# A planner's priorities from a table by the pair's place in its batch set, and high weights first in one form of the second layer

## The chip, the cores and the metric

The kernel runs on 1 core of one Trainium2 chip. The metric is device time in microseconds (us). Before the change the median of 3 runs is 901.65 us (898.36 to 903.74). The core's engines are TensorE (PE; its weight loads are listed apart as PEld), VectorE (DVE), ScalarE (ACT), GpSimd (POOL) and SyncE (SP), which here issues nearly all DMA transfers on one queue.

## What is computed

Attention with a threshold instead of a mask, then a mixture-of-experts layer on the tokens that a skip score lets through:

```python
# q, k, v: (8 batches, 8 heads, 576, 64); x: 4608 tokens of 512; 8 experts, 512 -> 1024 -> 512
scores = scale * np.matmul(q, k.transpose(0, 1, 3, 2))
thresh = np.max(scores, axis=-1, keepdims=True) - tau
scores = np.where(scores >= thresh, scores, -1000000000.0)
attn = softmax(scores)
x = (attn @ v) rearranged to tokens
do_compute = x @ w_skip > 0                  # the others leave as x
xc = x[do_compute]; logits = xc @ w_gate
e_idx = np.argmax(logits, axis=1); gate_w = softmax(logits) of that expert
for e in range(8):                            # the tokens of expert e
    h = np.maximum(xc[mask] @ w1[e], 0.0)
    y[mask] = gate_w[mask, None] * (h @ w2[e])
out[do_compute] = xc + y
```

## The kernel before

**Attention.** The work is cut into 32 pairs of heads (4 pairs a batch, 8 batches). A pair has 9 units of 128 query rows by 576 keys: four chunks of two units, and a last single unit that holds the remaining 64 rows of both heads. Each unit goes through the same steps. PE makes the scores (`S`, L537) into a PSUM tile `sps`, of which there are 3. DVE takes the row maximum (`mx`, L548), then the threshold of the chunk (`th`, L555). ACT takes the exponentials (`e`, L560). DVE compares and multiplies into `p` (`p`, L568), which frees the `sps` tile. ACT then copies a chunk's `p` as a high half in 16 bits (`ph`, L348, out `hla`), POOL subtracts to get the low half (`pl`, L619), SP sends both halves through DMA transposes (`tt`, L624, out `PTa`, 3 buffers), and PE multiplies with V (`av`, L687). The last unit is transposed on PE (L641) and split by ACT and DVE (L649, out `TM`).

**V of a batch.** SP loads it in six transfers into `vraw` (L399, L403, L406), one buffer. Two sums of its absolute values are taken (`fsum`: on DVE L432, or on ACT L430; the planner chooses the engine). From them a power of two is made (L440 to L471), by which V is scaled (L491, L494) and split into a high half `Vh` and a low half `Vl` (L502).

**Between the pairs.** SP loads q and k two pairs ahead (L373, L374, `KQ`) and ACT scales the keys (`qs`, L379). Finished token rows are stored (L858, L868). A finished pair's rows are turned on PE (L795) and multiplied with the gate's weights (L821). After every second batch DVE runs the gate (L920 to L1016, some 25 small steps) and POOL scatters the records (L1044): from pairs 10, 18 and 26 on and, for the last two batches, at the end.

**The order.** All these steps are handed to a planner (`Plan`) as operations with dependences, estimated durations, and a key. `Plan.run` goes forward in estimated time: of the operations that are ready on an engine within 0.1 us of each other, it issues the one with the smallest key. Instructions then stand on each engine in that order, and an engine that waits for one holds all behind it. The key is a number: 9 times the pair's number plus twice the chunk's, plus an offset by kind of step from the table `OFF`. The offsets lie between -6854 and 7967; the pair's part goes to 287. The gate's small steps are spread by `GS` (50.281) from one to the next.

**The experts.** At the end of attention the expert with the most tokens is chosen (L1095 to L1112), its weights are loaded (L333) and split into high and low parts (copies L350 and L348, subtractions `wl`, L1196, on DVE or POOL), its tokens are gathered (L337 with the numbers from L1148 and L1149) and turned (L1216), and its first layer runs (L1247). The code after `pl.run` is written in a fixed order: for each of the nine jobs, first layer (`layer1`, L1469), second layer (`layer2`, L1531, or for three jobs `layer2_t`, L1550, with the weights as the stationary operand), the split of the next weights (L1428 on ACT, L1429 on DVE and POOL), stores (L1509). All products are made of three: high times high, low times high, high times low.

Of the kernel before, what the change touches and what calls it, by code (L numbers as in the profile page):

```python
# [20 lines left out]
PSUM = bass.MemoryType.PSUM  # L21
# [4 lines left out]
S = 576  # L26
# [22 lines left out]
STEP = 2 * NM + 1  # L49
NBK = (NM + 1) * H + H // 2  # L50
NTL = NM * H
SPB = 3
# [7 lines left out]
TMB = 2  # L60
RING = 2
TD = 0.0
GS = 50.281
DU = 7
WRB = 4
LOOK = 0.1
# [3 lines left out]
LTO = {"PE": 0.08, "DVE": 0.0, "ACT": 0.0, "POOL": 0.01, "SP": 0.05}  # L70
DISS = 2.2
DLAT = 1.9
OFF = dict(
    gk=-2113.0, vm=619.2, tt2=3725.8, hi2=-664.7, lo2=-5330.0, eg=6314.5, L1m=-3010.0, ex=-2785.6, eav=102.1, ld=17.7, qs=-4430.6, S=-2220.1, mx=4043.6, th=-6854.0, e=-1838.1, p=-3039.7, ph=-893.6, pl=-1882.1, tt=-2108.6, av=4179.2, cp=-1831.1, x=1668.8, xw=-2128.1, row=4356.9, rsp=4714.0, init=2975.2, L1=7966.6, sc=-3459.1, d0=1027.8, phD=4238.9, v=1589.6, vsp=523.9, V2=-555.1,
)

class Op:
    def __init__(self, key, fn, eng, lat, lock):
# [16 lines left out]
class Plan:  # L95
# [7 lines left out]
        self.rings[name][1].append(list(ops))  # L103

    def op(self, key, fn, deps, eng, lat=None, lock=False):
        o = Op(key, fn, eng, lat, lock)
        for d in deps:
            if isinstance(d, tuple) and len(d) == 1:
                o.deps.append((d[0], True))
            elif isinstance(d, tuple):  # L110
                name, bufs = d
                al, fr = self.rings.setdefault(name, ([], []))
                if al:
                    o.deps.append((al[-1], True))
# [71 lines left out]
def attn_moe_kernel(ctx: ExitStack, tc: tile.TileContext, kq, vl, vt, tau, wg, w1, w2, out):  # L186
# [6 lines left out]
    cp = ctx.enter_context(tc.tile_pool(name="cp", bufs=1))  # L193
# [29 lines left out]
    att = ExitStack()  # L223
    ap_ = att.enter_context(tc.tile_pool(name="att", bufs=2))
    a1 = att.enter_context(tc.tile_pool(name="a1", bufs=1))
    ps_s = att.enter_context(tc.tile_pool(name="ps_s", bufs=SPB, space=PSUM))
    ps_t = att.enter_context(tc.tile_pool(name="ps_t", bufs=GPB, space=PSUM))
    ps_a = att.enter_context(tc.tile_pool(name="ps_a", bufs=1, space=PSUM))

    QKs = []  # L230

# [92 lines left out]
    pl = Plan()  # L324
# [1062 lines left out]
    att.close()  # L1387
    moe = ExitStack()
    mp = moe.enter_context(tc.tile_pool(name="moe", bufs=2, reuse_waits="tile"))
    ps_x = moe.enter_context(tc.tile_pool(name="ps_x", bufs=2, space=PSUM, reuse_waits="tile"))  # L1390
    ps_h = moe.enter_context(tc.tile_pool(name="ps_h", bufs=3, space=PSUM, reuse_waits="tile"))
    ps_y = moe.enter_context(tc.tile_pool(name="ps_y", bufs=3, space=PSUM, reuse_waits="tile"))

    class late:
        at, base = 0, None
# [142 lines left out]
    def layer2_t(j, w, side):  # L1538
# [2 lines left out]
        yt = mp.tile([P, NDT, TCAP], F32, name="yt", tag="yt", bufs=1)  # L1541
        for d in range(NDT):
            yp = ps_y.tile([P, 512], F32, name="yps", tag="yps")
            mm = [
                (w_[:, f, d * P : (d + 1) * P], h[:, f, 0:cap])
                for f in range(NFT)
                for (h, w_) in ((j.hh, wh), (j.hl, wh), (j.hh, wl))
            ]
            for i, (w_, h) in enumerate(mm):
                nc.tensor.matmul(yp[:, 0:cap], w_, h, start=(i == 0), stop=(i == len(mm) - 1))  # L1550
            nc.scalar.activation(yt[:, d, 0:cap], yp[:, 0:cap], AF.Copy)
            for s in side.get(d, ()):
                s()
# [130 lines left out]
    for k in range(1, len(jobs)):  # L1684
        j = jobs[k]
# [147 lines left out]
```

## Time and profile before

| | before |
|---|---|
| median of 3 runs | 901.65 us |
| lowest, highest | 898.36, 903.74 us |
| profiled execution | 897.73 us |
| its span, first to last instruction | 895.6 us |
| PE, DVE, ACT, POOL busy | 802.1, 692.3, 595.4, 573.4 us |
| mean granted TensorE clock | 0.966 |

Attention fills the first 600 us of the span, the handover to the experts lasts until 634 us, and the experts' layers run from there to the end. The profile is of one execution; it is read by stretches (busy time of each engine in a window), by waits (who waited for whom) and by engine in order of time. A wait's number is idle time of the waiting engine; it costs nothing where another engine sets the pace.

### The profile page before, as it was taken

The page shows a single profiled execution, that of the slowest core. Times are in us where ns is not written, and L with a number is a line of the kernel's source. Part 1 is how long each engine was busy: PE and PEld are TensorE (multiplying, and loading weights), DVE is VectorE, ACT ScalarE, POOL GpSimd, SP SyncE. Part 2 cuts the span into 40 slices and gives each one's busy share as a digit, 9 for nine tenths or more (in the row PEclk, how much of TensorE's full clock was granted, in tenths as well). Part 3 has the DMA queues.
Part 4 walks back from the last instruction along what each step waited for, and adds up shares of the span by engine and source line. Part 5 has one row for each costly group of instructions (what it writes and reads, how often), then busy time and mean ns, then how long its engine had stood idle before and what let it go on. Part 6 is the DMA issues. An engine that isn't in the chain of part 4 may idle for free. (4 is left out here: it accounts for less than half of the span.)

```text
span 895.6 us, 19554 instructions
## 1 busy us (share of the span) xinstructions
PE 802.1 (90%) x7294; PEld 679.0 (76%) x7294; DVE 692.3 (77%) x1294; ACT 595.4 (66%) x933; POOL 573.4 (64%) x379
## 2 busy tenths in 40 slices
PE   7799899898899888989988898975999999999997
PEld 5577787677677677777777776864968898999986
DVE  7789889989998798988888988895453554487782
ACT  5588888985987696797788779853243452454451
POOL 4567965975986494797676689756253455473463
PEclk9799999999999899999999999996799999999999
DMA  9699999999999999999999999987354635544540
GB/s 210 141 182 181 183 186 204 203 219 200 188 182 177 197 194 208 194 186 181 201 215 180 209 214 155 202 155 234 137 174 140 212 104 180 188 148 163 186 148 19
DMA packets 340031, 160.84 MB, mean 180 GB/s; under 512 B 311095, under 2 KB 311863, under 8 KB 339936
## 3 DMA queue, kind: packets, MB, share of 16 engines
q1 hardware_dynamic: 335312, 149.43, 81.8%
q0 software_dynamic: 4480, 10.15, 3.4%
q8 instruction: 59, 0.97, 0.5%
q14 instruction: 36, 0.29, 0.1%
q10 hardware_dynamic: 144, 0.00, 0.0%
HBM read 69.33 MB, written 15.21 MB: 94 GB/s over the span
## 5 line engine op out<-in xcount | busy, mean ns | idle before, releaser
L619 POOL TENSOR_TENSOR hla<-p,hla 128x1152 f16<-128x1152 f32 x128 | 304.4, 2379 | 121.5 <-ACT hla L348 109.3
L537 PE MATMUL sps<-KQ 128*128 128x288 f32 x1152 | 324.8, 426 | 37.7 <-DVE p L568 34.2
L537 PEld LDWEIGHTS sps<-KQ 128*128 128x128 f32 x1152 | 212.9, 195 | 100.6 <-PE avp L687 16.4
L560 ACT ACTIVATE ea<-sps,mx 128x576 f32<-128x576 f32 x288 | 206.8, 740 | 59.1 <-DVE mx L548 50.8
L548 DVE TENSOR_REDUCE mx<-sps 128x1 f32<-128x576 f32 x288 | 214.9, 751 | 34.7 <-PE sps L537 32.1
L568 DVE SCALAR_TENSOR_TENSOR p<-sps,tq,ea 128x576 f32<-128x576 f32 x256 | 200.1, 812 | 19.8 <-ACT ea L560 6.0
L348 ACT ACTIVATE hla<-p 128x1152 f16<-128x1152 f32 x128 | 148.8, 1162 | 29.2 <-DVE p L568 15.8
L687 PEld LDWEIGHTS <-PTa 128*128 128x128 f16 x3456 | 128.0, 99 | 36.5 <-issue 16.8
L687 PE MATMUL avp<-Vh,PTa 128*128 128x65 f16 (+1 forms) x2304 | 140.4, 199 | 16.0 <-ACT a L348 7.9
L687 PE MATMUL avp<-Vl,PTa 128*128 128x64 f16 (+1 forms) x1152 | 128.4, 198 | 6.1 <-POOL Vl L502 5.4
L1429 POOL TENSOR_TENSOR wl<-wr,wh 128x1024 fp32r<-128x1024 f32 x26 | 66.7, 2581 | 26.6 <-ACT wh L1428 18.7
L1509 POOL DMA_INDIRECT out<-o,ids x20 | 20.0, 998 | 80.8 <-DVE o L1508 27.1
L1469 PE MATMUL hps<-xh,wh 128*128 128x288 f32 (+4 forms) x224 | 69.1, 308 | 0.1
L1469 PE MATMUL hps<-xl,wh 128*128 128x288 f32 (+4 forms) x224 | 67.9, 303 | 0.0
L1469 PE MATMUL hps<-xh,wl 128*128 128x288 f32 (+4 forms) x224 | 67.8, 303 | 0.0
L1470 ACT ACTIVATE QK<-hps 128x288 fp32r<-128x288 f32 (+4 forms) x56 | 23.9, 426 | 60.8 <-PE hps L1469 60.2
L1428 ACT ACTIVATE wh<-wr 128x1024 fp32r<-128x1024 f32 x56 | 56.7, 1051 | 0.0
L1044 POOL DMA_INDIRECT lst<-rec,si x36 | 35.9, 998 | 31.6 <-DVE h L1255 17.0
L1429 DVE TENSOR_TENSOR wl<-wr,wh 128x1024 fp32r<-128x1024 f32 x30 | 50.2, 1689 | 6.9 <-ACT wh L1428 6.1
L348 ACT ACTIVATE a<-avp 64x65 f32<-64x65 f32 (+1 forms) x128 | 36.8, 301 | 20.1 <-PE avp L687 19.6
L1471 DVE SCALAR_TENSOR_TENSOR QK<-hps,QK 128x288 fp32r<-128x288 f32 (+4 forms) x56 | 26.2, 470 | 31.0 <-ACT QK L1470 29.0
L739 POOL TENSOR_TENSOR xb<-a,z 128x512 f32<-128x512 f32 x32 | 33.4, 1042 | 24.5 <-DVE z L730 10.7
(244 smaller groups left out, 1323.4 us busy)
## 6 DMA issues: line engine op xcount, KB each, us to landing
wr<-in_w SPq DMA_DIRECT2D x29, 1024.0 KB
KQ<-in_kq SPq DMA_DIRECT2D x32, 320.0 KB
KQ<-in_kq SPq DMA_DIRECT2D x32, 304.0 KB
vraw<-in_vl SPq DMA_DIRECT2D x32, 256.0 KB
out<-xb SPq DMA_DIRECT2D x32, 256.0 KB
PTa<-hla SPq DMA_TRANSPOSE x256
wn<-in_w SPq DMA_DIRECT2D x2, 1024.0 KB
vraw<-in_vt SPq DMA_DIRECT2D x8, 128.0 KB
```

The lines of the kernel that those rows point to most:

```text
L348: nc.scalar.activation(dst, src, AF.Copy)
L537: nc.tensor.matmul(ps[:, j, 0:HS], w, k[:, c0 : c0 + HS], start=True, stop=True, skip_group_check=True)
L548: nc.vector.tensor_reduce(T["mx", g][:, c, 0:1], bank(u), AX.XY, ALU.max, negate=True)
L560: nc.scalar.activation(e, bank(u), AF.Exp, bias=T["mx", g][:, c, 0:1])
L568: nc.vector.scalar_tensor_tensor(T["p", g, i][:, u].rearrange("p (a b) -> p a b", a=2), bank(u), T["tq", g][:, c : c + 1], T.pop(("e", g, ...
L619: nc.gpsimd.tensor_tensor(hl[:, lo0 : lo0 + w], T.pop(("p", g, i)).rearrange("p a b -> p (a b)"), hl[:, 0:w], op=ALU.subtract)
L687: nc.tensor.matmul(pv[:, o, 0:e], x[:, w_, :], y[:, vb, 0:e], start=not M and i % 2 + a + k == 0, stop=a == len(work) - 1 and k == 2, skip ...
L739: nc.gpsimd.tensor_tensor(T["x", b].rearrange("p c (h d) -> p c h d", d=D)[:, :, 2 * hp : 2 * hp + 2], T["a", g][:, 0:NM, :, 0:D], T["z", ...
L1044: sc = nc.gpsimd.indirect_dma_start(lst[:, :], bass.IndirectOffsetOnAxis(ap=G["si"][:, 0, t : t + 1], axis=0), G["rec"][:, t, :], None, bo ...
L1428: nc.scalar.activation(w[0][:, sl], rs, AF.Copy)
L1429: lo[q % 2].tensor_tensor(w[1][:, sl], rs, w[0][:, sl].bitcast(F32), op=ALU.subtract)
L1469: nc.tensor.matmul(hp_[:, 0:cap], w_, x, start=(i == 0), stop=(i == len(mm) - 1))
```

## The change

Four edits. First, a key no longer is a number. `OFF[kind]` gives a symbolic key, and `place` turns a sum of such keys into a priority by looking up the table `ORDER` at the pair's number modulo the length of the kind's row: rows of four depend on the pair's place in its batch, rows of two on even or odd pairs, rows of one are constant. The pair's and the chunk's number only choose the place; small additions such as `+ 0.1 * u` count no more. Keys without an `OFF` (the start, the second-layer weights, the steps planned ahead) stay numbers. Second, `GS` comes from the table as well and is 3.047e-10, so the steps of a gate share one priority. Third, the PSUM pools are opened in another order: in attention `ps_s` comes last, in the experts' stage `ps_y` first. Fourth, `layer2_t` takes all products with the high weights of an output block before those with the low weights, as `layer2` already does. No instruction is added or removed but for the planner's choice of engine for steps that can run on two.

```diff
-GS = 50.281
-OFF = dict(
-    gk=-2113.0, vm=619.2, tt2=3725.8, hi2=-664.7, ...
+ORDER = dict(
+    vm=(5384, 0, 0, 0,),
+    ld=(-3.456e+04, 1.596e+05, -1.641e+05, 6.358e+04,),
+    S=(-2.225e+05, -1.566e+05, -2.312e+04, -9.311e+04,),
...
+    GS=(3.047e-10,),
 )
+class Key:
+    def __init__(self, at=0.0, offs=()):
+        self.at, self.offs = at, tuple(offs)
...
+def place(key):
+    if not isinstance(key, Key):
+        return key
+    pair = int(max(key.at, 0)) // STEP
+    return sum(c * ORDER[n][pair % len(ORDER[n])] for n, c in key.offs) if key.offs else key.at
+OFF = {n: Key(0, [(n, 1)]) for n in ORDER}
+GS = OFF["GS"]
...
-        o = Op(key, fn, eng, lat, lock)
+        o = Op(place(key), fn, eng, lat, lock)
...
-    ps_s = att.enter_context(tc.tile_pool(name="ps_s", bufs=SPB, space=PSUM))
     ps_t = att.enter_context(tc.tile_pool(name="ps_t", bufs=GPB, space=PSUM))
     ps_a = att.enter_context(tc.tile_pool(name="ps_a", bufs=1, space=PSUM))
+    ps_s = att.enter_context(tc.tile_pool(name="ps_s", bufs=SPB, space=PSUM))
...
+    ps_y = moe.enter_context(tc.tile_pool(name="ps_y", bufs=3, space=PSUM, reuse_waits="tile"))
     ps_x = moe.enter_context(tc.tile_pool(name="ps_x", bufs=2, space=PSUM, reuse_waits="tile"))
     ps_h = moe.enter_context(tc.tile_pool(name="ps_h", bufs=3, space=PSUM, reuse_waits="tile"))
-    ps_y = moe.enter_context(tc.tile_pool(name="ps_y", bufs=3, space=PSUM, reuse_waits="tile"))
...
+            three = ((j.hh, wh), (j.hl, wh), (j.hh, wl))
             mm = [
                 (w_[:, f, d * P : (d + 1) * P], h[:, f, 0:cap])
+                for part in (three[0:2], three[2:])
                 for f in range(NFT)
-                for (h, w_) in ((j.hh, wh), (j.hl, wh), (j.hh, wl))
+                for (h, w_) in part
             ]
```

In the changed kernel all planned steps stand 64 lines further down (L399 is L463). The order of instructions differs nearly everywhere in attention; three places follow.

**SP, the load of V of batch 4** (pairs 14 and 15 before, the end of pair 12 in the change; `vraw<-in_vl` and `vraw<-in_vt` are V, `out<-xb` the stores of token rows, `PTa<-hla` transposes, `KQ` loads of q and k). Before:

```order
L624 DMA_TRANSPOSE PTa<-hla 128x9x128 x7
L403 DMA vraw<-in_vt 64x512
L406 DMA vraw<-in_vt 64x256
L624 DMA_TRANSPOSE PTa<-hla 128x9x128 x6
L399 DMA vraw<-in_vl 128x512
L624 DMA_TRANSPOSE PTa<-hla 128x9x128
L399 DMA vraw<-in_vl 128x512
L373 DMA KQ_109<-in_kq 64x1280
L374 DMA KQ_109<-in_kq 64x1216
```

and in the change:

```order
L688 DMA_TRANSPOSE PTa<-hla 128x9x128 x4
L463 DMA vraw<-in_vl 128x512 x2
L922 DMA out<-xb 128x512 x4
L467 DMA vraw<-in_vt 64x512
L470 DMA vraw<-in_vt 64x256
L463 DMA vraw<-in_vl 128x512 x2
L688 DMA_TRANSPOSE PTa<-hla 128x9x128 x14
```

The six transfers of V, which were spread over two pairs for batches 2, 4 and 6, stand together with the four stores between two transposes, for every batch from 2 to 7; the sums of V come 12 units after them where they came 6.

**DVE, the first gate** (pair 10; `ca` and `gw` are the gate's tiles, `vmx<-vraw` a sum of V, L568 the masks `p`). Before:

```order
L929 TENSOR_TENSOR ca<-lg,gw 128x72
L930 TENSOR_TENSOR ca<-lg,gw 128x72
L548 TENSOR_REDUCE mx_120<-sps 128x1
L432 TENSOR_REDUCE vmx<-vraw 128x1
L555 TENSOR_REDUCE tq_121<-mx_120 128x2
L440 TENSOR_REDUCE vmx<-vmx 128x1
L568 SCALAR_TENSOR_TENSOR p<-sps,tq_121,ea 128x576 x2
L933 TENSOR_TENSOR ca<-ca,ioem 128x72
L934 TENSOR_SCALAR gw<-lg 128x9
L972 TENSOR_REDUCE gw<-ca 128x9
L973 TENSOR_SCALAR rec<-tokp 128x9
```

and in the change:

```order
L993 TENSOR_TENSOR ca<-lg,gw 128x72
L994 TENSOR_TENSOR ca<-lg,gw 128x72
L612 TENSOR_REDUCE mx_120<-sps 128x1
L997 TENSOR_TENSOR ca<-ca,ioem 128x72
L998 TENSOR_SCALAR gw<-lg 128x9
L619 TENSOR_REDUCE tq_121<-mx_120 128x2
L1001 TENSOR_REDUCE gw<-ca 128x9
L1002 TENSOR_SCALAR gw<-gw 128x9
L632 SCALAR_TENSOR_TENSOR p<-sps,tq_121,ea 128x576 x2
L1005 TENSOR_TENSOR ca<-ioem,gw 128x9x8
```

The sum of V has left DVE here (in batches 3, 5 and 7 ACT now makes both sums, so DVE makes 5 of the 16 instead of 8), the gate begins half a pair earlier, and its steps are mixed more finely with the units' steps.

**DVE, the handover to the experts** (from the last mask `pm`, L568; `wl` are the low parts of the first expert's weights, `TM` the last unit's low half, `id` the numbers for the gather). Before:

```order
L568 SCALAR_TENSOR_TENSOR pm_117<-sps,tq_121,ea 128x576
L1196 TENSOR_TENSOR wl_8291<-wr,wh_8283 128x512
L1196 TENSOR_TENSOR wl_8309<-raw_8249,wh_8283 128x512
L1196 TENSOR_TENSOR wl_8309<-raw_8249,w_8339 128x512
L649 TENSOR_TENSOR TM_128<-sps,TM_128 128x640
L835 TENSOR_TENSOR lg<-lg,gps 128x64
L1148 CAST id_146<-rec_145 128x3
L1149 TENSOR_SCALAR id_146<-rec_145 128x3
```

and in the change:

```order
L632 SCALAR_TENSOR_TENSOR pm_117<-sps,tq_121,ea 128x576
L899 TENSOR_TENSOR lg<-lg,gps 128x64
L414 CAST wh_8246<-wr 128x512
L1260 TENSOR_TENSOR wl_8277<-wr,wh_8246 128x512
L899 TENSOR_TENSOR lg<-lg,gps 128x64
L713 TENSOR_TENSOR TM_128<-sps,TM_128 128x640
L1260 TENSOR_TENSOR wl_8356<-raw_8153,wh_8246 128x512 x2
L1260 TENSOR_TENSOR wl_8356<-raw_8153,w_8318 128x512
L1212 CAST id_146<-rec_145 128x3
L1213 TENSOR_SCALAR id_146<-rec_145 128x3
```

The last unit's low half has moved ahead of three of the subtractions, and the gather's numbers still stand behind them; POOL makes four of the eight subtractions instead of three, in a row.

## Rows read from the trace of the kernel before

**Rows 1.** Busy time by stretch: us, busy us of each engine (instructions), clock, DMA share, GB/s
```profile
200.00:300.00 100.00, 88.90 (x1002) 73.21 (x1000) 88.51 (x168) 79.28 (x123) 75.05 (x46) 0.98 1.09 189
...
600.00:650.00 50.00, 38.39 (x264) 33.91 (x263) 27.13 (x70) 15.35 (x31) 22.74 (x21) 0.71 0.61 189
...
740.00:780.00 40.00, 40.00 (x241) 35.97 (x241) 19.25 (x33) 14.99 (x26) 20.64 (x11) 1.00 0.58 194
```
**Rows 2.** Waits in attention, 30 to 600 us: who for whom, us in total, times, longest
```profile
PE sps L537 <- DVE p L568: 31.4, 46, 2.5
DVE mx L548 <- PE sps L537: 30.5, 65, 1.3
...
ACT KQ L379 <- DMA KQ<-in_kq: 14.8, 11, 3.6
...
PE avp L687 <- DMA PTa<-hla: 5.8, 8, 1.3
PE avp L687 <- POOL Vl L502: 5.4, 1, 5.4
```
**Rows 3.** Busy time by pair, columns as in rows 1: pairs 7, 10, 15, 23
```profile
138.10:156.60 18.50, 17.05 (x207) 14.34 (x206) 17.41 (x35) 16.40 (x26) 10.90 (x6) 1.00 1.09 212
...
189.00:213.30 24.30, 21.25 (x242) 17.88 (x241) 22.66 (x53) 17.37 (x29) 13.25 (x7) 0.93 1.08 193
283.30:306.50 23.20, 18.91 (x206) 15.65 (x205) 17.78 (x35) 17.10 (x29) 12.30 (x8) 0.89 1.14 182
...
434.80:455.50 20.70, 17.33 (x207) 14.38 (x206) 17.57 (x35) 16.59 (x29) 10.94 (x6) 1.00 1.16 196
```
**Rows 4.** Groups of instructions in attention: count, busy us, mean ns, idle before
```profile
L432 DVE TENSOR_REDUCE vmx<-vraw 128x1 f32<-128x1280 f32 x7 | 10.4, 1479 | 3.5 <-DMA vraw<-in_vl 3.5
...
L430 ACT ACTIVATE Vl<-vraw 128x1280 f16<-128x1280 f32 x7 | 8.8, 1262 | 0.0
```
**Rows 5.** In order of time, pair 15: SP's last load of V, and DVE and ACT
```profile
293.07 0.56 SPq L399 DMA_DIRECT2D vraw<-in_vl  x1
...
298.65 1.49 DVE L432 TENSOR_REDUCE vmx<-vraw 128x1 f32<-128x1280 f32 x1 [2.81 <-DMA vraw<-in_vl]
...
300.99 0.83 ACT L379 ACTIVATE KQ<-KQ,tpos 128x640 f32<-128x640 f32 x1 [3.59 <-DMA KQ<-in_kq]
```
**Rows 6.** In order of time: SP's longest run of transfers, PE's product; sizes (page)
```profile
178.31 0.56 SPq L858 DMA_DIRECT2D out<-xb  x1
178.97 0.87 SPq L399 DMA_DIRECT2D vraw<-in_vl  x2
...
181.18 9.30 SPq L624 DMA_TRANSPOSE PTa<-hla  x6
...
200.03 0.19 PE L687 MATMUL avp<-Vh,PTa 128*128 128x65 f16 x1
...
vraw<-in_vl SPq DMA_DIRECT2D x32, 256.0 KB
out<-xb SPq DMA_DIRECT2D x32, 256.0 KB
```
**Rows 7.** DVE, POOL and PE in order of time at the handover
```profile
608.27 7.20 DVE L1196 TENSOR_TENSOR wl<-wr,wh 128x512 fp32r<-128x512 f32 x1
...
607.87 2.40 POOL L619 TENSOR_TENSOR hla<-p,hla 128x1152 f16<-128x1152 f32 x1
...
613.88 1.04 POOL L739 TENSOR_TENSOR xb<-a,z 128x512 f32<-128x512 f32 x1
...
615.40 0.68 DVE L1196 TENSOR_TENSOR wl<-raw,wh 128x512 fp32r<-128x512 f32 x1
...
617.47 0.40 PE L687 MATMUL avp<-Vh,TM 128*128 128x130 f16 x2 [2.80 <-DVE TM L649]
...
626.39 0.93 PE L1216 MATMUL sps<-ident,xg 128*128 128x128 f32 x3
```
**Rows 8.** PE's waits in the experts' stage, 625 us to the end
```profile
PE yps L1550 <- POOL wl L1429: 1.9, 2, 1.2
```

More of the change, by code (lines that the diff above doesn't have):

```diff
@@ L72 @@
 DLAT = 1.9
-OFF = dict(
-    gk=-2113.0, vm=619.2, tt2=3725.8, hi2=-664.7, lo2=-5330.0, eg=6314.5, L1m=-3010.0, ex=-2785.6, eav=102.1, ld=17.7, qs=-4430.6, S=-2220.1, mx=4043.6, th=-6854.0, e=-1838.1, p=-3039.7, ph=-893.6, pl=-1882.1, tt=-2108.6, av=4179.2, cp=-1831.1, x=1668.8, xw=-2128.1, row=4356.9, rsp=4714.0, init=2975.2, L1=7966.6, sc=-3459.1, d0=1027.8, phD=4238.9, v=1589.6, vsp=523.9, V2=-555.1,
-)
+ORDER = dict(
+    gk=(4349, 1.58e+04, 0, 0,),
+    vm=(5384, 0, 0, 0,),
+    tt2=(613.7, 1.58e+04, -3.449e+04, -1512,),
+    hi2=(-4.346e+04, 3.034e+05, 3.133e+05, -5282,),
+    lo2=(562.8, -2.259e+04, -9.309e+04, -4.515e+04,),
+    eg=(-7406, -2.093e+05, 0, 0,),
+    L1m=(2.989e+05,),
+    ex=(-8.448e+04, 1.427e+04, -3.875e+04, -2e+04,),
+    eav=(-1.313e+05, -1.651e+04, 4.278e+04, 1.964e+04,),
+    ld=(-3.456e+04, 1.596e+05, -1.641e+05, 6.358e+04,),
+    qs=(1.122e+05, 1717, -9.452e+04, 1.214e+04,),
+    S=(-2.225e+05, -1.566e+05, -2.312e+04, -9.311e+04,),
+    mx=(5534, 2.237e+05, -6.53e+04, -6820,),
+    th=(-3.468e+04, 1.915e+05, -1.495e+05, 6.269e+04,),
+    e=(-1.451e+05, -6.782e+04, -2141, -1.003e+04,),
+    p=(-9031, -1.426e+04, -1.807e+05, -1.63e+05,),
+    ph=(-1322, 1.222e+05, 4.057e+05, -9.705e+04,),
+    pl=(-1.781e+05, 4.205e+04, 6250, -6.626e+04,),
+    tt=(-2.69e+05, 6405, -2703, 9.818e+04,),
+    av=(3.22e+05, 2.029e+04, 3.147e+04, 3.456e+04,),
+    cp=(1.287e+04, -3.512e+04, -6.049e+04, -1.725e+05,),
+    x=(-2.958e+04, -4.386e+04, 0.001192, 4.233e+04,),
+    xw=(2433, 1831, 1.558e+04, -1.251e+05,),
+    row=(-1594, 0, 0, 0,),
+    rsp=(-1.029e+05, 0, 0, 0,),
+    init=(-2.381e+05,),
+    L1=(-1.868e+05,),
+    sc=(-1.345e+05,),
+    d0=(-1.107e+04,),
+    v=(0.000848, 0, 0, -9374,),
+    vsp=(-0.0004024, 0, 0, -1.917e+05,),
+    V2=(0.002816, 0, 0, 0,),
+    GS=(3.047e-10,),
+)
@@ new lines, with __add__, __mul__, __sub__ @@
+class Key:
+    def __init__(self, at=0.0, offs=()):
+        self.at, self.offs = at, tuple(offs)
+    def __add__(self, x):
+        x = x if isinstance(x, Key) else Key(x)
+        return Key(self.at + x.at, self.offs + x.offs)
+    def __mul__(self, a):
+        return Key(self.at * a, [(n, c * a) for n, c in self.offs])
+    def __sub__(self, x):
+        return self + x * -1
+    def __rsub__(self, x):
+        return self * -1 + x
+    __radd__, __rmul__ = __add__, __mul__
+def place(key):
[3 more added lines that the diff above has]
+    return sum(c * ORDER[n][pair % len(ORDER[n])] for n, c in key.offs) if key.offs else key.at
```

## The prediction

> **What bounds the kernel now.** I read the stretches first [rows 1]. In the experts' stage PE is busy for the whole of a 40 us window: there only what stands on PE, or a wait of PE, changes the time. In attention no engine is full: in a window of 100 us PE is busy for 88.9 us and DVE for 88.5. Then the waits [rows 2]: PE waits 31.4 us for DVE's masks, DVE 30.5 us for PE's scores. The two are a ring through three `sps` tiles; a step of DVE or PE in that ring costs about what it lasts, and ACT, POOL and SP cost something only where one of the two waits for them. Third, the pairs [rows 3]: pair 7 takes 18.5 us, while pair 10 (first gate) takes 24.3 with DVE busy for 22.66, and pairs 15 and 23, which stand at the same place of a batch as pair 7, take 23.2 and 20.7 with DVE idle for 5.4 and 3.1. So the gate's pairs are bound by DVE, and pairs 15 and 23 by something that comes late. Fourth, these late things in order of time [rows 5], then the handover [rows 7] and PE's waits behind it [rows 8].
>
> The sum is made on the profiled execution, 897.73 us; the median of the three runs, 901.65, lies 3.92 above it, and I add that at the end.
>
> **A. Three sums of V leave DVE in the gate's pairs.** A sum takes 1.48 us on DVE and 1.26 on ACT [rows 4]. Batches 3, 5 and 7, whose sums are made in pairs 10, 18 and 26, now have both on ACT. DVE is full there, so 3 x 1.48 = 4.4 us go. ACT takes 3 x 1.26 = 3.8 us more and is busy for 17.37 of 24.3 us in pair 10 [rows 3]: 6.9 us of cover in each pair for 1.3. Were that cover gone, since ACT's next exponential stands behind the sum, the gain would be nothing. Bounds -4.4 and 0; I take -4.4, from the row of the full DVE.
>
> **B. V comes early enough in pairs 15 and 23.** In pair 15 SP issues the last load of V at 293.07, DVE waits 2.81 us for it until 298.65, and ACT waits until 300.99 for keys whose load stands behind it on SP [rows 5]; the clock of that pair is 0.89 [rows 3]. The order listing for SP shows why: that load stands six units ahead of its use, and in the change twelve. Against pair 7 the excess is 23.2 - 18.5 = 4.7 and 20.7 - 18.5 = 2.2, in sum -6.9. If keys rather than V set those ends, nothing goes: ACT waits 14.8 us for keys in all [rows 2], and nothing in the change puts them earlier. Bounds -6.9 and 0; I take -6.9, since both pairs lack only this against pair 7.
>
> **C. High weights first in `layer2_t`.** PE waits there twice for low parts from POOL, 1.9 us in sum [rows 8]. In the change two thirds of a block's products stand ahead of the first that needs a low part, so the wait goes: -1.9. Products are neither added nor taken away; PE is full there, and nothing hides a cost. Bounds -1.9 and 0.
>
> **D. V and the stores in one run.** This is what the change adds. Six times, once for each of batches 2 to 7, SP now issues four loads of 256 KB, one of 128, one of 64 and four stores of 256 KB [rows 6] (the small ones by their shapes, 64x512 and 64x256) between two transposes: 2240 KB, or 2.29 MB. At pair 7's 212 GB/s [rows 3] that is 10.8 us. Behind them on SP stand the transposes that PE's products need. The longest run before had 960 KB, from 178.31 to 181.08; the last of the six transposes behind it was issued by 181.18 + 9.30 = 190.48, and the first product that uses it ran at 200.03, a lead of 9.6 us, without a wait [rows 6]. So a run of 10.8 us is 1.2 too long in the worst case, while the order gives back some: behind the run the first products stand 11 units after their scores, where the same place had 9. Between 0 and 1.2 I take 0.6 for each, 6 x 0.6 = +3.6. The bound above: two transposes belong to a product, and at 9.30 / 6 = 1.55 each they use 3.1 of the lead, so 10.8 - 6.5 = 4.3 each, +25.8; below, 0.
>
> On this point the Trainium skill speaks against the change: by "DMA: Bandwidth & Descriptors", section "Queues, rings and completion order", descriptors of one ring are worked off in their order, so a transpose cannot overtake the loads ahead of it. The trace leaves it open: behind the run of 960 KB six transposes were issued within 9.30 us, 1.55 each, and no product waited for them [rows 6]; by the rule D would lie at its upper end, the sum at +12.6, which is the first rival below.
>
> **E. The handover.** PE waits 2.80 us there for `TM` [rows 7], which DVE made behind all its subtractions; in the change it stands ahead of three of four. That could give -2.8. Against it, the gather's numbers still stand behind all of them. One subtraction on DVE took 7.20 us from 608.27 where another took 0.68 at 615.40, and the hold lasted as long as POOL worked without a pause, from 607.87 to 613.88 + 1.04 = 614.92 [rows 7]. In the change POOL makes four subtractions in a row where it made three, and one more DVE step held so would put the numbers back by 7.20 - 0.68 = 6.5, and with them the gather and its first reader on PE, now at 626.39 [rows 7]. Between -2.8 and +6.5 I take 0.
>
> The Trainium skill has a rule for the hold, "SBUF — State Buffer", section "Who interferes with whom": a DVE instruction with two inputs in SBUF shares a port with GpSimd, and whoever issues first keeps it for its whole instruction. The trace agrees in kind but not in length: DVE was held across five POOL instructions, 7.0 us, not one of 2.40. By the rule's one instruction E would be -2.8 and the sum 2.8 lower.
>
> **F. The start.** PE waits 5.4 us once for the first V [rows 2]. Three more units of scores now stand ahead of that product, while the steps that make V come three to four units later on their engines. Bounds -5.4 (it is hidden) and +5.4 (it lasts twice as long); 0.
>
> **G. Everything else that moved in attention.** The kinds of steps come round in the same numbers on each engine, only their places differ. The ring's two waits are 31.4 + 30.5 = 61.9 us [rows 2]; a tenth either way, 6.2, bounds it, since the order on PE and DVE within a unit is the same. 0. The PSUM pools' order moves addresses alone: 0, and nothing in the trace bears on it, so it counts within G's bounds.
>
> Sum: -4.4 - 6.9 - 1.9 + 3.6 = -9.6, so 888.1 us on the profiled execution, and 888.1 + 3.9 = 892.0 against the median. All bounds together: -27.6 (874.1 against the median) and +43.9 (945.6).
>
> **Rivals.** *R1, slower: the runs of transfers stop PE.* If the lead is used up by the transposes themselves, D costs 4.3 for each run, 25.8: -4.4 - 6.9 - 1.9 + 25.8 = +12.6, so 914.2 us. It turns to slower when a run costs over 13.2 / 6 = 2.2 us. For it: the lead of 9.6 is shorter than 10.8, and PE's waits for `PTa` exist already, 8 of them [rows 2]. Against it: their longest is 1.3, and the run of 960 KB cost nothing. *R2, no change: the waits only move.* If what ACT waits for in pair 15 is keys [rows 5], and the gate's pairs lose DVE's sum but wait for PE instead, A and B give nothing, and C and D cancel nearly: 901.6. For it: the ring shows PE and DVE waiting for each other in like amounts, so a gain of one can become a wait of the other. *R3, the gate's pairs gain more.* The gate begins half a pair earlier and is mixed finer. If half of the excess of pair 10, (24.3 - 18.5) / 2 = 2.9, goes in each of the three pairs on top of A, the sum falls by 8.7 to -18.3: 883.3. Against it: DVE is full there, and the gate's own steps are as many as before. That the change does nothing is excluded: the orders differ nearly everywhere.
>
> **How the numbers follow.** A measurement of this kernel can tell about 0.5%, 4.5 us, from no change: faster is below 897.1, slower above 906.2. The forecast, 892.0, has 0.46; of that 0.37 is faster, 0.08 within, 0.01 slower, by the spread of E to G. R3 at 883.3 has 0.16, all faster. R2 has 0.20: 0.05 faster, 0.11 within, 0.04 slower. R1 has 0.18, of it 0.17 slower and 0.01 within. In sum 0.58 faster, 0.20 within, 0.22 slower. The forecast's own range is 884 to 902. For 8 in 10 the range goes from 877 (R3 less 6.2 for G) to 910, which takes in the part of R1 in which a run costs up to about 3.6 us.
>
> **What would show it.** A: with the sum gone from DVE, pairs 10, 18 and 26 last about 22.8, DVE still busy for over nine tenths. B: no wait of DVE or ACT for `vraw`; pairs 15 and 23 at 18 to 19 us. C: the wait of `layer2_t` for POOL gone. D: PE's waits for `PTa` below 10 us in attention and pairs 5, 9, 13, 17, 21 and 25 no longer than their neighbours; tens of microseconds there mean R1. E: no step of DVE of over 3 us at the handover, which stays at some 34 us from 600 on. If the pairs change by a microsecond each with none of these rows moving, G was the term that I had wrong.

## The result, and the profile after

The changed kernel takes 891.74 us (median of 15 runs, 882.61 to 898.52) against 901.36 before (15 runs): ratio 0.9876, 95% interval 0.9846 to 0.9907. A ratio and its interval leave out runs that are more than 1.5% above the fastest of the same kernel, so that they can differ from the quotient of the medians. The change is 9.6 us by the medians; the forecast was 892.0. In a second session the changed kernel had 889.11 (6 runs) against 901.54.

The execution that was profiled is the fastest of the 15, with a span of 880.8 us and a mean granted clock of 0.975. It must not be set against the one of before without care: of the 15 runs the seven with a clock of 0.972 or more took 882.6 to 892.4 us, the other eight 890.9 to 898.5. So I took a second profile of the same kernel (below, `after_again`, span 889.9). The table gives the length of each part, worked out from the starts of the pairs' first row maxima:

| part (us) | before | changed | changed, second profile |
|---|---|---|---|
| start and pairs 0 to 3 | 86.8 | 80.5 | 81.8 |
| pairs 4 to 9 | 102.2 | 104.7 | 104.3 |
| pairs 10 and 11 (gate) | 43.6 | 39.8 | 46.1 |
| pairs 12 to 15 | 73.8 | 68.7 | 68.4 |
| pairs 16 and 17 | 33.5 | 34.2 | 34.4 |
| pairs 18 and 19 (gate) | 43.2 | 41.2 | 39.8 |
| pairs 20 to 23 | 72.3 | 70.3 | 71.7 |
| pairs 24 and 25 | 33.1 | 34.7 | 34.7 |
| pairs 26 and 27 (gate) | 41.4 | 41.5 | 41.2 |
| pairs 28 to 31 | 74.4 | 76.2 | 75.7 |
| last maximum to first layer | 30.0 | 28.1 | 29.2 |
| experts | 261.2 | 260.9 | 262.5 |

Pairs 7, 10, 15, 23 and 30 in the changed kernel, columns as in [rows 1], the first four to be read beside [rows 3]:

```profile
132.10:149.30 17.20, 17.00 (x196) 14.24 (x195) 15.89 (x32) 15.07 (x24) 12.62 (x8) 1.00 1.13 196
185.20:207.60 22.40, 17.09 (x188) 14.19 (x188) 21.99 (x53) 15.65 (x25) 10.86 (x6) 1.00 1.11 203
276.80:293.70 16.90, 15.80 (x179) 13.48 (x178) 15.08 (x32) 14.30 (x20) 11.11 (x7) 1.00 1.10 207
420.30:439.40 19.10, 17.09 (x178) 14.37 (x177) 15.09 (x31) 14.96 (x23) 12.13 (x7) 0.91 1.21 189
548.50:569.70 21.20, 16.46 (x149) 12.75 (x148) 19.30 (x44) 13.23 (x21) 11.09 (x9) 0.92 0.76 127
```

Pairs 15 and 23 have lost 6.3 and 1.6 us, the gate's pair 10 lost 1.9; pair 30, at 16.3 before, is new among the long ones. The waits from 30 to 600 us, in the form of [rows 2], and below them PE's wait in `layer2_t`, which answers to [rows 8]:

```profile
DVE mx L612 <- PE sps L601: 41.3, 72, 3.6
PE sps L601 <- DVE p L632: 35.1, 33, 2.8
PE avp L751 <- DMA PTa<-hla: 5.7, 10, 1.6
ACT KQ L443 <- DMA KQ<-in_kq: 2.4, 3, 1.5
...
PE yps L1616 <- POOL wl L1493: 1.4, 2, 1.0
```

Three things are to be seen here. PE's waits for transposes have not grown in sum (5.8 before), though 2.0 us of them now stand in pair 9, where there were none. ACT's waits for keys fell from 14.8 to 2.4, which no step of the prediction had. And the ring's own waits grew from 61.9 to 76.4.

### The profile page after: what moved, and what is told of

It reads as the page before. It is cut to its first block, busy times and chain, and to the rows that moved or that the text cites. A ratio compares the mean times of both kernels' runs of the same rounds, so it can differ in the third digit from the quotient of the medians.

```text
span 880.8 us, 19512 instructions
## 1 busy us (share of the span) xinstructions
PE 791.0 (90%) x7294; PEld 670.2 (76%) x7294; DVE 686.9 (78%) x1290; ACT 601.9 (68%) x939; POOL 575.7 (65%) x380
## 5 line engine op out<-in xcount | busy, mean ns | idle before, releaser
L601 PEld LDWEIGHTS sps<-KQ 128*128 128x128 f32 x1152 | 209.5, 193 | 114.1 <-issue 30.7
L751 PE MATMUL avp<-Vh,PTa 128*128 128x65 f16 (+1 forms) x2304 | 138.1, 199 | 10.2 <-DMA PTa<-hla 6.9
L1573 POOL DMA_INDIRECT out<-o,ids x20 | 20.0, 998 | 80.5 <-DVE o L1572 26.8
L1108 POOL DMA_INDIRECT lst<-rec,si x36 | 36.1, 1004 | 33.5 <-DVE tabp L1368 16.1
L1535 DVE SCALAR_TENSOR_TENSOR QK<-hps,QK 128x288 fp32r<-128x288 f32 (+4 forms) x56 | 26.1, 469 | 31.0 <-ACT QK L1534 30.8
L412 ACT ACTIVATE a<-avp 64x65 f32<-64x65 f32 (+1 forms) x128 | 37.0, 302 | 17.9 <-PE avp L751 16.6
L566 POOL TENSOR_TENSOR Vl<-vraw,Vh 128x1024 f16<-128x1024 f32 (+1 forms) x23 | 44.6, 1946 | 2.3 <-ACT Vh L412 2.3
```

What stands on the lines that cost most here:

```text
L412: nc.scalar.activation(dst, src, AF.Copy)
L566: (nc.gpsimd if e == POOL else nc.vector).tensor_tensor(T["Vl", b][:, ts], vraw[:, ts], Vh[:, ts, 0:D], op=ALU.subtract)
L601: nc.tensor.matmul(ps[:, j, 0:HS], w, k[:, c0 : c0 + HS], start=True, stop=True, skip_group_check=True)
L751: nc.tensor.matmul(pv[:, o, 0:e], x[:, w_, :], y[:, vb, 0:e], start=not M and i % 2 + a + k == 0, stop=a == len(work) - 1 and k == 2, skip ...
L1108: sc = nc.gpsimd.indirect_dma_start(lst[:, :], bass.IndirectOffsetOnAxis(ap=G["si"][:, 0, t : t + 1], axis=0), G["rec"][:, t, :], None, bo ...
```

## The experiments

All kernels whose names begin with `b_` are the kernel before, those with `a_` the changed one. Where single operations move, the planner's choice is replaced by a written list of all its 2994 operations in issue order, with their engines, so that nothing else changes:

```diff
     def run(self, look):
-        free, cand = {}, {}
...
+        for w in SEQ.split():
+            o, e = self.ops[int(w[1:])], dict(P="PE", D="DVE", A="ACT", G="POOL", S="SP")[w[0]]
+            o.on = e
...
+                o.fn()
```

### The same kernel again

> The changed kernel itself, a second look and a standard for the other runs on this chip. If the gain lies in the order, it shows again at the same places: pair 1 begins at about 25.4 us, pairs 15 and 23 last 17 to 19 us, and the time is 890 to 893 us. If part of what the first profile shows was only where TensorE's clock happened to dip, the pairs with a clock below 1 stand elsewhere and single pairs differ from the first profile by 1 to 2 us at the same order, while the sum of the pairs stays within 5 us.

889.11 us (879.08 to 897.6), ratio 0.9801 (0.9759 to 0.9842). Pair 1 began at 25.85, pairs 15 and 23 took 16.6 and 19.6. But pair 10, with the same instructions in the same order, took 28.3 instead of 22.4. The pairs 10 and 18 of this profile:

```profile
186.10:214.40 28.30, 21.31 (x188) 17.12 (x188) 22.59 (x55) 16.68 (x27) 11.63 (x7) 0.83 0.88 173
335.10:357.50 22.40, 17.08 (x188) 14.19 (x188) 22.00 (x54) 15.65 (x24) 10.86 (x6) 1.00 1.15 187
```

A gate's pair thus has two lengths, and which one comes goes with the clock: 1.00 or 0.83. PE's rows in that pair 10, with one of DVE, tell what it did before:

```profile
190.64 3.58 PE L601 MATMUL sps<-KQ 128*128 128x288 f32 x8 [2.03 <-DVE p L632]
...
195.19 2.22 DVE L1053 TENSOR_TENSOR co<-cnt,eoff 128x8 f32<-128x8 f32 x1
...
197.90 0.93 PE L859 MATMUL gps<-ident,xb 128*128 128x128 f32 x4 [2.49 <-DVE cnt L1057]
...
202.78 2.16 PE L601 MATMUL sps<-KQ 128*128 128x288 f32 x8
...
212.06 3.70 PE L601 MATMUL sps<-KQ 128*128 128x288 f32 x8 [2.47 <-DVE p L632]
```

Eight score products take 2.16 us at the upper level (2.4 GHz), and 3.58 and 3.70 behind waits of 2.03 and 2.47 us; the granted clock of these two stretches was 0.59, and behind the same two waits in the first profile it was 1.00. The clock is not all: with PE late, a gate step that took 0.15 us in the first profile (L1053) fell under a subtraction of POOL and lasted 2.22, and PE waited 2.49 us for what follows it instead of 0.71. The first profile is the exception: the four kernels below that have the beginning of pair 10 in the same order (`a_burst2`, `a_gate`, `a_gather`, `a_best`) all took 3.87 us for the eight products behind that first wait. The second part of the expectation holds in kind: single pairs differ by up to 6 us with no change of the order, more than the 1 to 2 I wrote, and the last maximum came 6.4 us later, more than the 5 allowed for the sum of the pairs.

### The start

The written list is the changed kernel's up to a cut in the planner's time, then that of before, without what was issued already; the engines follow the list. Three cuts:

```diff
-SEQ = before
+SEQ = changed[first 109 operations (30 us), 172 (45 us) or 314 (75 us)] + rest of before
```

> The kernel before, with the operations that the planner of the changed kernel issues in its first 30 us in the changed order, and all the rest in the order of before. Theory (start): the 5 us by which pair 1 begins earlier belong to the order of the start alone and stay to the end: pair 1 at about 25.4 us instead of 30.4, the later pairs as before, the time 5 to 6 us below before, 895 to 896. Rival (the waits come back): pair 1 begins earlier, but pairs 1 to 4 grow by what was saved, and the time is within 2 us of before.

901.12 us, ratio 0.999 (0.9967 to 1.0013): nothing. Pair 1 began at 26.1, then took 26.0. PE's wait had only moved behind the seam, where the list goes over to the order of before (26 to 52 us):

```profile
PE avp L798 <- POOL Vl L613: 5.3, 1, 5.3
```

> As b_start, but the changed order is kept for the planner's first 45 us instead of 30, so that the steps that scale V of batch 0 and make its low part stand in the changed order and on the changed engines too; the rest is in the order of before. In b_start PE still waited 5.3 us for the low part of V on POOL, a pair later. Theory (the start's gain hangs on V's steps): that wait is gone, pairs 0 to 2 take 54 to 55 us instead of 60.7, and the time is 5 to 6 us below before, 895 to 896. Rival (the waits come back): pairs 1 to 4 grow again by as much, within 2 us of before.

901.91 us, ratio 0.9996 (0.9975 to 1.0017). Pairs 0 and 1 now had the changed kernel's lengths and that wait was gone, but pair 2 took 24.0 at a clock of 0.86:

```profile
44.90:68.90 24.00, 19.61 (x204) 16.30 (x203) 16.23 (x30) 15.82 (x24) 10.88 (x6) 0.86 1.03 172
```

> As b_start and b_start45, with the changed order kept for the planner's first 75 us, that is to the end of pair 3; the rest is in the order of before. With 45 us the first two pairs took 16.4 and 19.5 us as in the changed kernel, but pair 2 took 24.0 instead of 17.8, with 2.8 us of PE's waits for the transposes and a clock of 0.86. Theory (that was the seam: the start's gain stays where the changed order goes on): pairs 0 to 3 take 71 to 73 us instead of 77.8, and the time is 5 to 6 us below before, 895 to 896. Rival (the gain is given back wherever the order of before begins): the pair behind the seam, 4 or 5, takes 4 to 6 us more than 16.8, and the time is within 2 us of before.

895.68 us, ratio 0.9945 (0.9913 to 0.9977), 4.9 us less than before in its session. Pair 2 was at 17.8, and no pair behind the seam took it back at once (pairs 4 and 5: 16.9 and 18.1). In its profile pairs 0 to 3 took 74.5 us, 3.3 less than before and above the 71 to 73 expected; pairs 0 and 1 were at the lower clock there (0.91 and 0.82). So the order of the first four pairs is worth about 5 us by the medians (2.1 to 7.8 by the interval), and two cuts that were too short show that half of such an order is worth nothing: what one pair gains the next loses where its own loads and sums stand in the old places.

### The sums of V

Three times, at the same place of the list:

```diff
-L432 DVE TENSOR_REDUCE vmx<-vraw 128x1
+L430 ACT ACTIVATE Vl<-vraw 128x1280
```

> The kernel before, in which three of the sixteen sums of V (the second of batches 3 and 5, the first of batch 7, in pairs 10, 18 and 26) are made on ACT instead of DVE, at the same place of the order. Theory (term A): DVE is full in those pairs, each gets 1.5 us shorter, 4.4 in sum, about 897. Rival (DVE's time there is not what the pairs wait for): the pairs stay at 24.3, 24.2 and 23.1 within half a us, and the time is within 2 us of before.

898.88 us, ratio 0.9981 (0.9959 to 1.0003), a gain that is not clear of zero. Pairs 10, 18 and 26:

```profile
190.70:213.80 23.10, 21.29 (x243) 17.86 (x242) 21.62 (x53) 18.64 (x31) 13.38 (x7) 0.93 1.05 201
339.60:362.30 22.70, 20.20 (x246) 17.10 (x246) 21.32 (x53) 18.93 (x32) 13.44 (x8) 1.00 1.06 183
486.70:512.80 26.10, 21.28 (x236) 17.97 (x235) 22.16 (x51) 19.81 (x32) 13.25 (x7) 0.93 1.16 202
```

Two of the three gave about what the theory says (24.3 to 23.1, 24.2 to 22.7), the second of them with the clock at 1.00 where it had 0.93. The third became longer by 3.0: there two gate steps that took 0.82 and 0.30 us before fell under subtractions of POOL and lasted 2.08 and 2.36.

### V's loads

On SP, for batch 4, and in the same way for batch 6 (line numbers of before):

```diff
 L399 DMA vraw<-in_vl 128x512 x2
+L403 DMA vraw<-in_vt 64x512
+L406 DMA vraw<-in_vt 64x256
+L399 DMA vraw<-in_vl 128x512 x2
 L373 DMA KQ_105<-in_kq 64x1280
 L374 DMA KQ_105<-in_kq 64x1216
 L624 DMA_TRANSPOSE PTa<-hla 128x9x128 x6
```

> The kernel before, with one move on SP: the last three of the five load operations of V (four transfers) of batches 4 and 6 stand directly behind the first two, as they do in the changed kernel; everything else in the order of before. Theory (term B): pair 15 goes from 23.2 to about 18.5 us and pair 23 from 20.7 to about 18.5, no wait for V there, 6.9 us less in sum, about 894.5. Rival (keys): ACT's wait for keys in pair 15 stays, the two pairs give 0 to 2 us, and the time is 900 to 901.

899.08 us, ratio 0.9963 (0.994 to 0.9986). Pairs 15 and 23 did fall to 18.2, 0.3 below the 18.5 of pair 7 by which term B measured them; but pair 13 went from 16.1 to 20.1 and pair 21 from 16.7 to 19.4. The waits in pair 13:

```profile
ACT KQ L490 <- DMA KQ<-in_kq: 3.7, 1, 3.7
DVE p L679 <- ACT ea L671: 3.0, 1, 3.0
PEld L798 <- DMA PTa<-hla: 2.0, 1, 2.0
PE avp L798 <- DMA PTa<-hla: 1.9, 1, 1.9
```

The keys stood right behind the run of V's loads. ACT, waiting for them, held the exponentials behind it. So the next kernel has V's loads behind those keys, where the changed kernel has them:

```diff
 L624 DMA_TRANSPOSE PTa<-hla 128x9x128 x4
-L399 DMA vraw<-in_vl 128x512 x2
 L373 DMA KQ_105<-in_kq 64x1280
 L374 DMA KQ_105<-in_kq 64x1216
 L624 DMA_TRANSPOSE PTa<-hla 128x9x128 x3
+L399 DMA vraw<-in_vl 128x512 x2
+L403 DMA vraw<-in_vt 64x512
+L406 DMA vraw<-in_vt 64x256
+L399 DMA vraw<-in_vl 128x512 x2
 L624 DMA_TRANSPOSE PTa<-hla 128x9x128 x3
 L373 DMA KQ_106<-in_kq 64x1280
```

> The kernel before with all six transfers of V of batches 4 and 6 at the place where the changed kernel has them, behind the last transposes of pairs 12 and 20, in one run; everything else in the order of before. In b_v_early, where they stood just ahead of the keys of pairs 15 and 23, pairs 15 and 23 fell to 18.2 us, but ACT waited 3.7 us for those keys in pairs 13 and 21 and these grew from 16.1 and 16.7 to 20.1 and 19.4. Theory (the keys behind the run of loads took the gain away): with the keys ahead of the run, pairs 13 and 21 stay at 16 to 17.5 us and pairs 15 and 23 at about 18.2, 6 to 7 us less than before in sum, about 894. Rival (any run of 1.2 MB costs the pair that it stands in 3 us): pairs 13 and 21 are at 19 to 20 us with waits for the transposes or for the keys of pairs 16 and 24, and the time is 898 to 900.

896.92 us, ratio 0.9925 (0.9901 to 0.9949), by the ratio that is 6.8 us below before (4.6 to 8.9). Pairs 13, 14 and 15:

```profile
253.50:269.60 16.10, 15.42 (x158) 13.12 (x158) 14.99 (x28) 13.88 (x21) 14.85 (x11) 1.00 1.04 207
269.60:288.20 18.60, 15.66 (x177) 13.19 (x176) 14.40 (x27) 13.44 (x18) 10.90 (x6) 1.00 1.16 204
288.20:306.40 18.20, 17.30 (x207) 14.42 (x206) 17.39 (x35) 16.74 (x29) 10.95 (x6) 1.00 1.06 188
```

Pairs 13 and 21 stayed at 16.1; pairs 14 and 22 took 1.3 and 1.6 more, waiting 2.3 and 2.5 us for the keys behind. The same load of 1.2 MB costs its pair 2.7 to 4.0 us ahead of the keys that are needed next, and the next pair 1.3 to 1.6 behind them.

### Twice the stores in each run of transfers

```diff
                 nc.sync.dma_start(out[r0 : r0 + P, :], T["x", b][:, t, :])
+                if b < B - 2:
+                    nc.sync.dma_start(again[t * P : (t + 1) * P, :], T["x", b][:, t, :])
```

> The changed kernel, in which each of the 24 stores of token rows of batches 0 to 5 is issued twice, the second time to a scratch area, so that each of the six runs of transfers has 3.3 instead of 2.25 MB and 14 instead of 10 issues. Theory (the runs are hidden, what is left of term D is nothing): PE's waits for the transposes stay below 10 us and the time is within 2 us of the changed kernel. Rival (the lead of the transposes is used up, the first rival of the prediction): 1.05 MB at 0.2 MB a us are 5 us for each run, and the time grows by 6 to 29 us, with PE's waits for the transposes up by as much.

902.37 us, ratio 1.0011 (0.9988 to 1.0034): by the medians some 13 us above the changed kernel on the same chip. PE's waits for the transposes, 30 to 585 us, and pair 14, which took 18.2 before the addition:

```profile
PE avp L752 <- DMA PTa<-hla: 13.8, 18, 2.1
...
266.80:290.10 23.30, 19.51 (x177) 15.26 (x177) 17.14 (x30) 15.34 (x23) 11.13 (x7) 0.85 0.99 176
```

PE's waits for the transposes are 9.2 us above the 4.6 in the second profile of the changed kernel, some 1.5 for each run. The theory fails, and the time is in the rival's range: the runs of the changed kernel cost little or nothing, and 1.05 MB more in each does cost. Where between the two the cost begins was not tried. Not all of the 13 us is waiting for transposes: pairs 10 and 18 were both at the lower clock (0.87) here, and the experts' stage, which these stores do not touch, took 265.6 us where it took 262.5.

### The other two edits

The third and the fourth edit of the change (the pools' order, and the products of `layer2_t`), put into the kernel before as they stand.

> The kernel before with the other two edits alone: the order of products in the second layer that has the weights stationary, and the order in which the PSUM pools are opened. Theory of the prediction (term C and the pools): PE's 1.9 us of waits for POOL in that layer go, 1.9 us less in the experts' stage, pools nothing. Rival (by the trace of the changed kernel): only 0.5 us of the wait goes, and the stage from the first layer to the end stays at 261 us. Either way the time is within 2.5 us of before; it tells whether the pools do more.

900.56 us, ratio 0.9985 (0.9962 to 1.0009). PE's wait in `layer2_t`, 630 us to the end, and where it falls, from the changed kernel:

```profile
PE yps L1552 <- POOL wl L1429: 1.4, 2, 1.0
...
784.21 0.95 PE L1616 MATMUL yps<-QK,wl 128*128 128x288 f32 x6
786.12 0.54 PE L1616 MATMUL yps<-QK,wl 128*128 128x288 f32 x2 [0.96 <-POOL wl L1493]
```

Half a microsecond, as the trace of the changed kernel said. PE gets through six of a block's eight low products and waits for the last two: the late part is POOL's last, and it stood near the end of a block in the old order too.

### The gates

In the changed kernel's pair 10 these two steps of DVE, of 72 and 9 elements a partition, last 2.05 and 2.36 us, and behind the second of them PE's scores wait for the masks that follow (DVE, POOL and PE in order of time):

```profile
194.03 2.05 DVE L1060 TENSOR_TENSOR ca<-ca,co 128x72 f32<-128x72 f32 x1
...
202.76 2.36 DVE L1076 TENSOR_SCALAR si<-si 128x9 int32<-128x9 int32 x1
...
193.61 4.72 POOL L683 TENSOR_TENSOR hla<-p,hla 128x1152 f16<-128x1152 f32 x2 [6.05 <-ACT hla L412]
...
202.73 2.37 POOL L683 TENSOR_TENSOR hla<-p,hla 128x1152 f16<-128x1152 f32 x1 [1.46 <-ACT hla L412]
...
189.70 2.18 PE L601 MATMUL sps<-KQ 128*128 128x288 f32 x8 [2.02 <-DVE p L632]
...
206.28 2.18 PE L601 MATMUL sps<-KQ 128*128 128x288 f32 x8 [2.46 <-DVE p L632]
```

Both end when the subtraction of POOL under which they began ends. PE's other wait in this pair, 2.02 us, is over at 189.70, before the first of the two steps begins at 194.03 and while POOL was idle (6.05 us until 193.61): it lies behind the gate's small steps themselves. The expectation below puts it down to the first step, and that is wrong. The move, twice a gate, on DVE:

```diff
-TENSOR_TENSOR ca<-ca,co 128x72
 SCALAR_TENSOR_TENSOR p<-sps,tq,ea 128x576 x2
+TENSOR_TENSOR ca<-ca,co 128x72
```

> The changed kernel with two moves on DVE in each of the three gates of pairs 10, 18 and 26: the step that adds the offsets to the ranks (the sum into ca from ca and co) stands behind the next two masks instead of ahead of them, and so do the two integer steps that make the slot's parts. In the changed kernel these two small steps last 2.05 and 2.36 us instead of 0.2, as long as POOL is in its subtraction, and PE waits 2.0 and 2.5 us for the masks behind them. Theory (DVE held by POOL is what makes the gate's pairs long): the holds still happen but end within 0.6 us, PE's two waits go, each gate's pair falls from 22.4 to 28 us to 20 or less, TensorE's clock no longer falls there, and the time is 880 to 885. Rival (the wait moves to the next maximum or the ring takes it): the pairs lose under 1 us each and the time stays within 3 us of the changed kernel.

883.46 us (6 runs), ratio 0.9797 (0.9758 to 0.9836). Pairs 10, 18 and 26 took 23.0, 21.4 and 21.5:

```profile
185.60:208.60 23.00, 19.54 (x190) 15.66 (x190) 19.82 (x53) 16.34 (x26) 10.92 (x6) 0.93 1.01 187
330.60:352.00 21.40, 17.89 (x190) 14.70 (x190) 19.08 (x54) 16.38 (x26) 10.85 (x6) 1.00 1.11 183
474.20:495.70 21.50, 17.98 (x191) 14.71 (x191) 19.17 (x55) 16.47 (x26) 10.86 (x6) 1.00 1.06 182
```

The second integer step is back at 0.16 us and the first takes 0.58; the sum still lasts 0.94 to 1.6. PE's wait of 2.46 us in pair 10 fell to 0.25. The wait of 2.03 at the beginning of the pair stayed, and behind it the clock fell, as in the changed kernel's second profile. Pairs 18 and 26 are 1.0 us shorter than the changed order's at the upper clock (22.4, and 22.5 in `a_gather` below), not the whole holds; no pair came to the theory's 20 or less. The time lies in the theory's range, 6 to 8 us below the changed kernel's two medians, but the interval of the ratio all but coincides with the changed kernel's in the second session (0.9759 to 0.9842). That one of PE's waits goes is shown; the gain in time is not, by this run alone.

### The gather, and all together

On POOL at the handover (line numbers of the changed kernel); on DVE, in the same way, the conversion of the gather's numbers stands ahead of its last subtraction instead of behind it:

```diff
 L1260 TENSOR_TENSOR wl<-wr,wh 128x512 x2
+L401 DMA xg<-out,id 128x512 x2
+L401 DMA xg<-out,id 64x512
 L1260 TENSOR_TENSOR wl<-wr,wh 128x512
 L1260 TENSOR_TENSOR wl<-raw,w 128x512
-L401 DMA xg<-out,id 128x512 x2
-L401 DMA xg<-out,id 64x512
```

> The changed kernel with one move at the handover: POOL gathers the first expert's tokens (with the numbers' load and conversion ahead of it) before its last two subtractions of the weights' low parts, instead of behind them. In the changed kernel the numbers were ready at 604.4 us and the gather began at 606.9. Theory (the gather sets the handover): the gather and the first layer begin 2 to 2.5 us earlier, 887 to 889 where the changed kernel has 889 to 892. Rival (the low parts come later and hold the first layer instead): the first layer begins within half a us of where it did, no gain, or 1 to 2 us lost.

884.94 us (6 runs), ratio 0.9829 (0.9792 to 0.9866). From the last maximum to the first layer it took 26.7 us, and 27.3 in the last kernel below, which has the same move; with the changed order it took 28.1 and 29.2, and 28.5 and 29.4 in `a_burst2` and `a_gate`. So a gain of 1 to 2 us at the handover is shown. The rest of the 4 to 7 us by which the median lies lower is not; it overlaps with the changed kernel's interval.

The last kernel adds the gates' moves and, on DVE in pair 30:

```diff
-L1002 TENSOR_SCALAR gw<-gw 128x4
 L619 TENSOR_REDUCE tq<-mx 128x2
 L612 TENSOR_REDUCE mx<-sps 128x1
 L632 SCALAR_TENSOR_TENSOR p<-sps,tq,ea 128x576 x2
+L1002 TENSOR_SCALAR gw<-gw 128x4
```

> The changed kernel with the moves of a_gate (gates of pairs 10, 18 and 26), the move of a_gather, and the same kind of move in pair 30, where a small gate step of DVE (128x4) lasted 2.34 us instead of 0.15 under a subtraction of POOL and PE waited 2.8 us: it stands behind the next two masks. Theory (each hold that PE waits for costs its own length and now and then a stretch at the lower clock): pair 30 falls from 21.2 to 17 to 18.5 us, the gates' pairs are 21 to 23 as in a_gate, and the time is 876 to 880. Rival (pair 30's length comes from something else, as the end of the batches' work): it stays at 20 to 21 us and the time is that of a_gate, 883, less what the gather gives.

879.02 us (6 runs, 874.06 to 883.58), ratio 0.9757 (0.9716 to 0.9799): 10 to 13 us below the changed kernel's medians, the fastest version here: 19 of the changed kernel's 21 runs were longer than the longest of these six. Pairs 18 and 26 took 21.4 as in `a_gate`, but pair 10 took 25.6 with its clock at 0.87, outside the 21 to 23 that I expected. Pair 30, and the gate's step in it:

```profile
550.00:567.60 17.60, 14.96 (x148) 12.04 (x147) 17.18 (x44) 13.13 (x21) 10.53 (x7) 1.00 0.91 158
...
562.82 0.16 DVE L1113 TENSOR_SCALAR gw<-gw 128x4 f32<-128x4 f32 x1
```

The step went from 2.34 us to 0.16 and the pair from 21.2 to 17.6. PE's wait for the masks behind the step went from 2.78 to 0.68, and the eight score products after it from 3.59 to 2.21 us, since the clock no longer fell there (0.92 for the pair before, 1.00 now): together 3.5 of the 3.6.

## Why the prediction was right, and where its steps were not

The sign and the range held, but the sum of the steps is right only in part. That the median came out within 0.3 us of the forecast is luck: terms that were wrong stood against each other, and the second session's median was 2.6 us lower with no change of the kernel.

- **A, -4.4: too large, and its mechanism holds only in part.** Alone it gave -1.7 us (from -3.7 to +0.3): 1.2 and 1.5 less in two pairs, 3.0 more in the third. In the changed kernel the three pairs took 69.2 and 74.0 us in the two profiles, against 71.6 before, so the term is not to be seen there. The step that failed is that a DVE that is full gives back what is taken from it; it does so only if the gate's next small step does not come to lie under a POOL instruction.
- **B, -6.9: right in place and size.** Pairs 15 and 23 lost 7.9 us in sum in the first profile and 7.6 in the second (16.9 and 19.1, 16.6 and 19.6, each a little outside the 18 to 19 forecast), and alone the move gave 6.8. Three details were wrong. That nothing in the change puts the keys earlier is not so: ACT's waits for them went from 14.8 to 2.4 us (3.4 in the second profile), and `b_v_early` shows that without the right place among the keys half of the gain comes back as waits. The twelve units between load and sum did not appear as time: in the changed kernel, the last two of V's loads were issued from 254.10 to 255.12 and the sum ran at 261.00, some 6 us later, about as before (293.07 to 298.65). What is earlier is the whole chain: the sum runs in pair 14, not 15, and V is scaled from 296.3 instead of 311.3. And pair 7, by which the excess was measured, lay behind the same spread loads, those of batch 2: it too became shorter, 17.2 after 18.5.
- **C, -1.9: wrong, 0.5.** I took the first product with a low part for the one that waits; it is the last two of a block's eight.
- **D, +3.6: little or nothing.** PE's waits for `PTa` did not grow in sum (5.8, then 5.7 and 4.6), though 2.0 and 1.5 us of them came in pair 9, behind a run. The term even had the runs too small: in three of the six, two stores of last units of 128 KB each (L932, from 177.79 in pair 9) stand between the four stores and V's loads, which makes 2.55 MB. `a_burst2` shows that the cost which the first rival named exists: with 1.05 MB more for each run some 13 us are lost, of which the profile shows 9.2 as PE's waits for transposes, and the ratio to before was 1.0011.
- **E, 0: -0.7 to -1.9.** The wait for `TM` went (-2.8), and the gather came to wait for POOL instead, which began it 2.5 us after its numbers were ready (604.38 to 606.89; 1.3 in the second profile). I had looked for that on DVE. A long step came there too, but elsewhere: a cast of 128x512 (L414) lasted 3.22 us from 595.60, where another took 0.47.
- **F, 0: wrong, -5.** The step that failed is that two opposite tendencies cancel: PE's wait for V's low part did go, and about the bound of -5.4 is what came. The clock has a part in it, which I had left out. Pairs 0 and 1 took 41.9 us before at 0.84 and 0.83; in the first profile they took 35.9 at 1.00, but 37.8 in `b_start75`, `a_gate` and `a_gather`, which have the same order and a clock of 0.91 and 0.82 to 0.83. So some 4 us are gained at the lower clock as well, and 2 more only where the clock stays up.
- **G, 0: about +6, at the edge of its 6.2.** Pairs 4 to 9, 16 and 17, 24 and 25, and 28 to 31 are longer by 2.5 or 2.1, 0.7 or 0.9, 1.6, and 1.8 or 1.3. Pair 30's 21.2 is a gate step under POOL. The others, pairs 8 and 24 above all (15.6 before, 17.5 to 18.0 now), I did not take apart; whether the runs of D have a part in them is open.

A, B and C were taken at -13.2 and came to about -9; D and G at +3.6 and came to about +6; F brought -5 and E about -1 that were not in the sum. A, B, C and F are sizes from kernels with that one part, E and G from the parts of the profiles; the gate's new order and the rest of G were not tried alone. Of the rivals, R2 (the waits only move) is what two of the partial orders did, though not the whole. R3 did not come: with A it had 4.4 us for each of the gate's pairs, and none lost more than 1.9. `a_gate` brought the three to 65.9 us in sum, 5.7 below before, by other means than mixing finer.

## What to carry to other kernels

A priority table's gain is in whole stretches of order: a load moved ahead of its use helps only if what stands behind it on the queue is not needed sooner, and half a moved order can be worth nothing. Before a small step is put between two large ones, look at what the neighbouring engine is doing then: a step of 0.2 us can stand for 2.4 on the path. And where the same kernel shows two clocks, compare several profiles of it before a pair's length is put down to the change.

## What the runs showed of the hardware

**A small DVE step can last as long as POOL's instruction.** A sum of 128x72, an integer step of 128x9 and a scale of 128x4 lasted 2.05, 2.36 and 2.34 us under a subtraction of 2.38, and 0.15 to 0.22 elsewhere. The Trainium skill, "SBUF — State Buffer", section "Who interferes with whom", has it that steps of DVE with two inputs in SBUF, and `tensor_scalar` in some modes, contend with GpSimd, and that the one that comes second is blocked for the other's whole instruction; these rows agree, one instruction each, while the 7.20 us of [rows 7], over five of them, stay unexplained by it.

**A wait of 2 us can cost PE 1.5 more.** Behind waits of 2.03 and 2.47 us, eight score products took 3.58 and 3.70 us instead of 2.16, at a granted clock of 0.59; in the first profile of the same kernel, behind waits of 2.02 and 2.46, they took 2.18 both times at 1.00. Behind the first of these waits the clock fell in five of the six profiles that have it. What decides between the two is open. The 15 runs spread over 16 us, the shorter ones mostly at the higher mean clock, so for a kernel like this one the mean granted clock of a run is to be read beside its time.
